# Packed attention and SwiGLU on one core: batch 0 as a written program, with plain fp32 products in its first four chunks

## The chip, the core and the metric

The kernel runs on one core of a Trainium2 chip. The kernel uses five engines, each with a queue of instructions of its own: TensorE (matmuls; the profile calls them PE, and the loads of the stationary operand PEld), VectorE (DVE), ScalarE (ACT), GpSimd (POOL) and SyncE (SP, which here issues nearly all DMA loads and stores). They wait for each other through semaphores. The metric is the device time of one execution in microseconds, lower is better.

## The reference

Eight batches of 576 tokens with 8 heads of 64 dimensions, and 32 pack queries per head and batch. Two attentions follow each other, then a SwiGLU layer:

```python
def sm_attn(qq, kk, vv):
    s = scale * np.matmul(qq, kk.transpose(0, 1, 3, 2))
    s = s - np.max(s, axis=-1, keepdims=True)
    a = np.exp(s)
    a = a / (np.sum(a, axis=-1, keepdims=True) + 1e-09)
    return np.matmul(a, vv)

p_packed = sm_attn(p, k, v)              # per head: 32 x 64
out = sm_attn(q, p_packed, p_packed)     # per head: 576 x 64
x = out, heads side by side              # 4608 tokens x 512
g = x @ w_gate                           # 512 x 1536
silu = g * (1.0 / (1.0 + np.exp(-g)))
return (silu * (x @ w_val)) @ w_out      # 1536 x 512
```

q, k, v and p arrive as fp32. The three weights arrive as 8-byte floats; the chip converts them to fp32 itself.

## The kernel before

**Folding.** The second attention ends with a product by the 32 packed values of each head, and the layer begins with a product by the gate and value weights. The kernel multiplies the two small factors first: M = (packed values) x (gate and value weights), per batch and per chunk of 128 of the 1536 hidden features (`m_part`, which does two chunks, a pair k, at once: `by_head`, L179). Then gate and value are products of M with the attention weights a2 alone (`gv_chunk`, L465). A chunk has a half a (256 tokens of an even batch) and a half b (the other 320); each half takes one PSUM tile for the gate and one for the value. ScalarE takes the silu of the gate tile (L472), VectorE multiplies it with the value tile (L478, and L481 for 64 tokens that are kept for a later product). The product h goes through the output weights into four PSUM accumulators.

**Precision.** A product is done either plainly in fp32 (each matmul shows as two records in the trace) or by three products of fp32r operands: both factors are split into a high part (a cast to fp32r, on ScalarE) and a low part (a subtraction, on VectorE), and low x high, high x low and high x high are added in PSUM. M is split into mh (L438) and ml (L421), a2 into a2h (L413) and a2l (L414). The output products of batches 1 to 7 are of three terms too (`out_mm`, L486), with output weights that are split once (`split_wout`, L144 and L145). Those of batch 0 are plain (`outs` in batch 0, L624).

**Batch 0 is different.** While it runs, the weights are converted: 12 chunks of gate and value weights (`convert_w`) and 6 pairs of chunks of output weights (`convert_wout`), a tile of 128 x 1024 each. A conversion (`f64_convert`) is two ScalarE passes (L111, L112) and then three VectorE passes (L113, L114, L115). It is a generator, so that its five steps can be put between other work one at a time. Beside this, batch 0 holds the whole attention of batch 1 (`aux_of`: scores, exponentials, transposes, packing, second scores and softmax), as each later batch holds that of its successor.

**Loads.** Raw weights, k and q of every batch go through one group of four buffers (`io_tile`). A load can be issued when the last reader of the tile that had its buffer is done.

**What sets the order.** TensorE's order is that of the program text throughout (the outer `manual_schedule`). In the preparation and in batch 0, VectorE's and ScalarE's order is that of the text too (the inner one). SP's order is chosen by the framework's planner. In batch 0 the text is a loop over the 24 halves: products of the half, its silu, some steps of conversions (`between`), its multiply, then the output products of the half five before (`LAG = 5`). M of pair k + 1 comes in the last half of pair k. Work in the list `late` (exponentials) goes behind a half's silu. After the loop come the last five output products, M of batch 1's first pair and the first two splits of output weights; the other ten splits lie in batch 1, two in each of five of its chunks.

## Time and profile before

| | |
|---|---|
| median of three runs | 796.53 us (795.73 to 796.65) |
| the profiled execution | 796.16 us |
| its span | 794.4 us |
| TensorE busy | 750.8 us (95%) |
| VectorE busy | 457.5 us (58%) |
| ScalarE busy | 376.2 us (47%) |
| first product of batch 0 | 23.29 us after the start of the span |
| last output product of batch 0 ends | 151.03 us |

The span is what the trace covers, from the first to the last instruction; the 1.8 us between it and the execution's time lie around it. A busy share is an average over the whole span: the slices of the page show TensorE at 40 to 90% in the first seven of 40 and above 90% after them. Matmuls are pipelined, so that the duration of one matmul (0.3 to 0.6 us in the groups) is longer than the distance to the next; where a stream of matmuls is to be priced, the chain of waits gives the distance, as it counts each stretch of time once. The granted clock of TensorE is printed for each stretch as a share of full speed.

### The profile page before, as it was taken

The page shows a single profiled execution, that of the slowest core. Times are in us where ns is not written, and L with a number is a line of the kernel's source. Part 1 is how long each engine was busy: PE and PEld are TensorE (multiplying, and loading weights), DVE is VectorE, ACT ScalarE, POOL GpSimd, SP SyncE. Part 2 cuts the span into 40 slices and gives each one's busy share as a digit, 9 for nine tenths or more (in the row PEclk, how much of TensorE's full clock was granted, in tenths as well). Part 3 has the DMA queues.
Part 4 walks back from the last instruction along what each step waited for, and adds up shares of the span by engine and source line. Part 5 has one row for each costly group of instructions (what it writes and reads, how often), then busy time and mean ns, then how long its engine had stood idle before and what let it go on. Part 6 is the DMA issues. An engine that isn't in the chain of part 4 may idle for free.

```text
span 794.4 us, 14060 instructions
## 1 busy us (share of the span) xinstructions
PE 750.8 (95%) x5750; PEld 590.0 (74%) x5750; DVE 457.5 (58%) x1002; ACT 376.2 (47%) x670; POOL 2.0 (0%) x13
## 2 busy tenths in 40 slices
PE   7478988999999999999999999999999999999998
PEld 5355555578777887878778787777888777888886
DVE  5785885565585554755475554754566454653434
ACT  3477673364462645464262643645362552643331
POOL 0000000000000000000000000000000000000000
PEclk9799999999999999999999999999999999999999
DMA  9564745320301212020211103010101000010001
GB/s 356 217 215 160 285 159 179 113 64 12 118 1 67 66 41 87 25 92 4 81 47 67 65 3 126 1 55 3 67 2 53 15 3 1 1 55 1 1 1 66
DMA packets 20000, 59.08 MB, mean 74 GB/s; under 512 B 5984, under 2 KB 7008, under 8 KB 17376
## 3 DMA queue, kind: packets, MB, share of 16 engines
q1 hardware_dynamic: 19792, 58.12, 20.5%
q8 instruction: 45, 0.74, 0.4%
q14 instruction: 19, 0.16, 0.1%
q10 hardware_dynamic: 144, 0.07, 0.0%
HBM read 48.69 MB, written 9.49 MB: 73 GB/s over the span
## 4 chain that ended last, share of the span: by engine, by line
PE 71%; ACT 10%; DVE 3%; issue 2%; ACTq 0%; DVEq 0%
PE gv L465 31%; PE acc L486 25%; PE aux L179 6%; PE aux L486 4%; ACT L472 4%; PE aux L349 2%; PE acc L624 2%; ACT sg L472 1%; DVE ml L421 1%; ACT mh L438 1%; ACT L297 1%; ACT hh L89 1%; ACT L392 1%; PE aux L284 1%; ACT s L392 1%
## 5 line engine op out<-in xcount | busy, mean ns | idle before, releaser
L465 PE MATMUL gv<-a2h,ml 128*128 128x256 f32 (+1 forms) x768 | 178.0, 313 | 24.3 <-ACT sg L472 13.7
L465 PEld LDWEIGHTS gv<-a2h,ml 128*128 128x128 f32 x768 | 129.7, 191 | 60.9 <-ACT sg L472 20.6
L472 ACT ACTIVATE sg<-gv 128x256 f32<-128x256 f32 x192 | 78.7, 410 | 192.0 <-PE gv L465 144.6
L465 PE MATMUL gv<-a2l,mh 128*128 128x256 f32 (+1 forms) x768 | 166.1, 298 | 0.0
L465 PE MATMUL gv<-a2h,mh 128*128 128x256 f32 (+1 forms) x768 | 165.7, 297 | 0.0
L478 DVE TENSOR_TENSOR hf<-gv,sg 128x256 f32<-128x256 f32 x168 | 70.7, 421 | 134.1 <-PE gv L465 117.8
L486 PE MATMUL acc<-wo_h,hl 128*128 128x512 f32 x336 | 136.6, 406 | 0.0
L486 PE MATMUL acc<-wo_l,hh 128*128 128x512 f32 x336 | 132.2, 393 | 0.0
L486 PE MATMUL acc<-wo_h,hh 128*128 128x512 f32 x336 | 131.6, 392 | 0.0
L465 PEld LDWEIGHTS gv<-a2l,mh 128*128 128x128 f32 x768 | 125.1, 191 | 0.3 <-DVE a2l L414 0.3
L465 PEld LDWEIGHTS gv<-a2h,mh 128*128 128x128 f32 x768 | 125.3, 192 | 0.0
L89 ACT CAST hh<-hf 128x256 fp32r<-128x256 f32 x168 | 67.8, 404 | 113.4 <-DVE hf L478 113.4
L95 DVE TENSOR_TENSOR hl<-hf,hh 128x256 fp32r<-128x256 f32 x168 | 71.1, 423 | 84.0 <-ACT hh L89 83.5
L486 PEld LDWEIGHTS acc<-wo_h,hl 128*128 128x128 f32 x336 | 63.2, 188 | 42.5 <-issue 34.4
L421 DVE TENSOR_TENSOR ml<-aux,mh 128x512 fp32r<-128x512 f32 (+1 forms) x96 | 61.2, 679 | 29.8 <-ACT mh L438 29.8
L486 PEld LDWEIGHTS acc<-wo_h,hh 128*128 128x128 f32 x336 | 63.1, 188 | 14.5
L486 PEld LDWEIGHTS acc<-wo_l,hh 128*128 128x128 f32 x336 | 63.3, 188 | 7.7
L179 PE MATMUL aux<-w,ppt 64*32 64x512 f32 (+1 forms) x768 | 52.7, 602 | 5.0 <-DVE w L115 3.3
L438 ACT CAST mh<-aux 128x512 fp32r<-128x512 f32 (+1 forms) x96 | 50.9, 583 | 8.1 <-PE aux L179 5.4
L472 ACT ACT_TABLE_LOAD x35 | 44.9, 1283 | 12.4 <-issue 11.6
L624 PE MATMUL acc<-wo_f,h 128*128 128x512 f32 x96 | 45.9, 598 | 0.9 <-DVE wo_f L115 0.9
L624 PEld LDWEIGHTS acc<-wo_f,h 128*128 128x128 f32 x96 | 16.6, 189 | 17.0 <-issue 15.2
(130 smaller groups left out, 631.2 us busy)
## 6 DMA issues: line engine op xcount, KB each, us to landing
st<-in_wgv SPq DMA_DIRECT2D x12, 1024.0 KB, 6.4
k_t<-in_kT SPq DMA_DIRECT2D x16, 576.0 KB, 4.8
q_t<-in_qT SPq DMA_DIRECT2D x16, 576.0 KB, 5.0
out<-ot SPq DMA_DIRECT2D x36, 256.0 KB, 2.1
v_t<-in_vq SPq DMA_DIRECT2D x6, 1280.0 KB, 5.7
st<-in_wout SPq DMA_DIRECT2D x6, 1024.0 KB, 4.8
v_t<-in_v SPq DMA_DIRECT2D x2, 1024.0 KB, 10.0
p_t<-in_pT SPq DMA_DIRECT2D x7, 64.0 KB, 1.8
```

Of the source, the lines that this page charges most:

```text
L89: e.copy(dst, src)
L95: lo.tensor_tensor(dst_l, src, dst_h.bitcast(F32), op=ALU.subtract)
L179: nc.tensor.matmul(outs[par][32 * hp : 32 * hp + 32], lhs(r, hp), rhs(r, hp), start=True, stop=True)
L349: nc.tensor.matmul(p_p[D * par : D * par + D, NP * hp : NP * hp + NP], v_t[:, par, hp, k, :], a1[:, par, hp, k, :], start=(k == 0), stop=( ...
L392: pin(nc.scalar.activation(x, x, AF.Exp, scale=SCALE))
L421: nc.vector.tensor_tensor(*lows.pop(0), op=ALU.subtract)
L438: nc.scalar.copy(mh[at], src)
L465: nc.tensor.matmul(pg[:, :n], m_[:, g, f, s * P : (s + 1) * P], a_[:, g, off : off + n], start=(i == 0), stop=(i == 5),)
L472: nc.scalar.activation(sg[:, :n], pgs[0][:, :n], AF.Silu)
L478: nc.vector.tensor_tensor(hf, pgs[1][:, o : o + 256], sg[:, o : o + 256], op=ALU.mult)
L486: nc.tensor.matmul(acc[:, :], h_[:, c : c + P], w_[fc // 2][:, fc % 2], start=(fc == 0 and i == 0), stop=(fc == NFC - 1 and i == 2),)
L624: nc.tensor.matmul(accs[2 * is_b + c], half(i)[:, c * P : c * P + P], wos[fc // 2][:, fc % 2], start=(fc == 0), stop=(fc == NFC - 1),)
```

## The change

The order of batch 0 is written out as text. In `run`, every word is one step: `g5` the products of half 5, `S5` its silu, `H5` its multiply, `O5` its output products, `M2.0` or `M2.2` M of pair 2 for its first or for both chunks (pair 6 stands for the first pair of batch 1), `L` the low parts of M, `W7:2` and `V2:1` so many steps of the conversion of gate and value chunk 7 and of output pair 2, `w7` and `v2` their loads, `a0` a low part of a2, `p3` a split of an output weight, `x` the next step of batch 1's attention, `q1` and `k2` loads of batches 1 and 2.

- Halves 0 to 7 (chunks 0 to 3) are products of one plain fp32 term: M is copied to SBUF without a split, and a2 is used as it comes from its transposes (`a2f`). From chunk 4 on there are three terms, in the order high x high, high x low, low x high. The parts of a2 are made ahead of half 7.
- The first four halves change their order: a of chunk 0, a of chunk 1, b of chunk 0, b of chunk 1. M of the first two pairs is done chunk by chunk.
- The two ScalarE passes of a conversion stand behind the silu of a half, ahead of the half in which VectorE's passes follow.
- An output product comes four halves after its half, and directly behind the products (and the M) of a half.
- The loads have two groups (rings) of two buffers, and SP's order is that of the text. The first load of an output weight and k of batch 1 move ahead of gate and value chunk 3 and of v of batch 1.
- 18 warm-up matmuls stand ahead of the first product in place of 10.
- Six output weights are split at the end of batch 0, the other six in chunks 1 to 6 of batch 1, one in each.

The diff, cut:

```diff
-    def io_tile(shape, dtype, name):
-        return pool.tile(shape, dtype, tag="io", bufs=4, name=name)
-    def f64_load(src):
-        st = io_tile([P, 1024, 2], I32, "st")
+    def io_tile(ring, shape, dtype, name):
+        return pool.tile(shape, dtype, tag=f"io{int(ring)}", bufs=2, name=name)
+    def f64_load(src, ring):
+        st = io_tile(ring, [P, 1024, 2], I32, "st")
...
+        sts[fc] = f64_load(wgv[fc], 0 if fc in (2, 5, 8, 10) else 1)
...
+        sts["out", k] = io_tile(k in (0, 3), [P, 1024, 2], I32, "st")
...
+        k_t = io_tile(0, [P, 2, NHP, HS], F32, "k_t")
         if b == 0:
-            qs[b] = io_tile([P, 2, NHP, HS], F32, "q_t")
+            qs[b] = io_tile(0, [P, 2, NHP, HS], F32, "q_t")
...
+            qs[b] = io_tile(1, [P, 2, NHP, HS], F32, "q_t")
...
+    def m_part(b, k, fcs, low=True, parts=("mh", "ml")):
+        plain = len(parts) == 1
         if (b, k) not in ms:
-            ms[b, k] = tuple(pool.tile([P, NPAR, 2, 2 * P], F32R, tag=t, bufs=2, name=t) for t in ("mh", "ml"))
-        mh, ml = ms[b, k]
+            dt = F32 if plain else F32R
+            ms[b, k] = tuple(pool.tile([P, NPAR, 2, 2 * P], dt, tag=t, bufs=2, name=t) for t in parts)
+        mh = ms[b, k][0]
...
+            if not plain:
+                lows.append((ms[b, k][1][at], src, mh[at].bitcast(F32)))
...
-        with tc.manual_schedule(engines={mybir.EngineType.DVE, mybir.EngineType.Activation}):
+        with tc.manual_schedule(
+            engines={mybir.EngineType.DVE, mybir.EngineType.Activation, mybir.EngineType.SP}
+        ):
...
-            load_v(1)
-            load_w(3)
-            load_k(1)
...
-            m_part(0, 0, slice(0, 1), low=False)
+            m_part(0, 0, c0, parts=("mh",))
             s2_max(0, c0)
             s2_exp(0, c0)
-            m_lows()
-            next(w1)
-            next(w1)
+            next(s2)
+            load_k(1)
+            load_wout(0)
+            warm_up(18)
+            steps(1, 2)
+            a2f = pool.tile([P, NPAR, S], F32, tag="a1", bufs=1, name="a2f")
+            def back(c):
+                for par in range(NPAR):
+                    nc.vector.transpose(a2f[:, par, c * HS : (c + 1) * HS], st2[0][0][:, c, par])
             s2_sums(0, c0)
             s2_scale(0, c0)
-            low = s2_back(0, 0)
-            run_all(s2)
-            warm_up(10)
-            low()
-            s2_max(0, c1)
-            s2_exp(0, c1)
-            next(w1)
-            next(w1)
-            s2_sums(0, c1)
-            s2_scale(0, c1)
-            low = s2_back(0, 1)
+            back(0)
...
+            order = [(0, 0), (1, 0), (0, 1), (1, 1)] + [divmod(i, 2) for i in range(4, 2 * NFC)]
+            PLAIN = 2
+            held = {}
+            def gv(i):
+                fc, is_b = order[i]
+                off, n = (NA, NB) if is_b else (0, NA)
+                k, f = divmod(fc, 2)
+                if k < PLAIN:
+                    terms = ((ms[0, k][0], a2f),)
+                else:
+                    (mh, ml), (ah, al) = ms[0, k], a2[0]
+                    terms = ((mh, ah), (mh, al), (ml, ah))
+                held[i] = [ps_gv.tile([P, 512], F32, tag="gv", name="gv") for _ in range(2)]
+                for s in range(2):
+                    todo = [(m_, a_, g) for m_, a_ in terms for g in range(NPAR)]
+                    for j, (m_, a_, g) in enumerate(todo):
+                        nc.tensor.matmul(
+                            held[i][s][:, :n], m_[:, g, f, s * P : (s + 1) * P], a_[:, g, off : off + n],
+                            start=(j == 0), stop=(j == len(todo) - 1),
+                        )
...
+            def a2_high():
+                s2_a2(0)
+                for c in range(2):
+                    at = (slice(None), slice(None), slice(c * HS, (c + 1) * HS))
+                    nc.scalar.copy(a2[0][0][at], a2f[at])
+            def a2_low(c):
+                at = (slice(None), slice(None), slice(c * HS, (c + 1) * HS))
+                nc.vector.tensor_tensor(a2[0][1][at], a2f[at], a2[0][0][at].bitcast(F32), op=ALU.subtract)
...
-            gv_chunk(0, 0, False, nothing, half(0), first_a)
...
+            gv(0)
+            s2_max(0, c1)
+            s2_exp(0, c1)
+            run("S0 W1:2 V0:1 W1:1 w3")
+            load_v(1)
+            run("M0.1")
+            s2_sums(0, c1)
+            run("V0:1 H0")
+            s2_scale(0, c1)
+            back(1)
+            run("g1 V0:1 S1 W2:1 H1 g2 V0:1 S2 W2:1 V0:1 w4 H2 g3 S3 W3:1 x O0 W2:1 H3 W2:1 W3:1 x O1 W2:1 w5 v1 M1.0")
+            run("O2 g4 S4 W4:1 W3:2 H4 g5 S5 W4:1 W3:1 w6 M1.1 W4:1 H5 x g6 S6 W5:1 W4:2 w7 H6 W5:1")
+            a2_high()
+            run("a0 g7 S7 V1:1 a1 W5:1 H7 W5:2 v2 M2.2 O3 V1:1 W6:1 L W6:1")
+            for words in (
+                "g8 S8 W7:2 V1:2 W6:1 H8 V1:1 w8 W6:1 O4",
+                "g9 S9 V2:2 W6:1 w9 H9 W7:1 V2:1 O5",
+                "g10 S10 x x W7:1 H10 W7:1 v3 O6",
+                "g11 S11 W8:1 M3.2 H11 V2:1 L W8:1 V2:1 w10 O7",
+                "g12 S12 W9:2 W8:1 H12 W8:1 x O8",
+                "g13 S13 V3:2 W8:1 H13 W9:1 V3:1 v4 O9",
+                "g14 S14 x W9:1 H14 W9:1 w11 O10",
+                "g15 S15 W10:1 M4.2 H15 V3:1 L W10:1 V3:1 q1 x O11",
+                "g16 S16 W11:2 W10:1 H16 W10:1 x O12",
+                "g17 S17 V4:2 x W10:1 H17 W11:1 V4:1 v5 O13",
+                "g18 S18 x W11:1 H18 x W11:1 O14",
+                "g19 S19 M5.2 H19 V4:1 L V5:2 V4:1 k2 x O15",
+                "g20 S20 x H20 V5:1 O16",
+                "g21 S21 x H21 x V5:1 O17",
+                "g22 S22 x H22 V5:1 O18",
+                "g23 S23 M6.2 H23 x L O19",
+                "O20 x p0 O21 x p1 O22 p2 p3 O23 p4 p5",
+            ):
+                run(words)
...
-                    if b == 1 and fc > 1 and count[0] in (3, 7):
-                        split_wout(fc - fc % 2 + count[0] // 7) if fc % 2 == 0 else None
+                    if b == 1 and 1 <= fc <= 6 and count[0] == 7:
+                        split_wout(fc + 5)
```

More of the change, by code (lines that the diff above doesn't have):

```diff
@@ L449, in h_split, with gv_chunk @@
         return hh, hl
-    def gv_chunk(b, fc, is_b, fill, kept=None, between=lambda: None):
+    def gv_chunk(b, fc, is_b, fill):
         odd = b % 2
@@ L474, in gv_chunk @@
             late.pop(0)()
-        between()
-        hf = pool.tile([P, 256], F32, tag="hf", bufs=2, name="hf") if kept is None else kept
+        hf = pool.tile([P, 256], F32, tag="hf", bufs=2, name="hf")
         o, o4 = (64, 0) if is_b and odd else (0, 256)
@@ L574, in tile_pack_attention_swiglu, with steps @@
             s1 = s1_post(0, True)
-            w0, w1 = convert_w(0), convert_w(1)
+            conv = {}
+            def steps(key, n=9):
+                if key not in conv:
+                    conv[key] = convert_wout(key[1]) if isinstance(key, tuple) else convert_w(key)
+                for _ in range(n):
+                    next(conv[key], None)
             for _ in range(4):
                 next(s1)
-            for _ in range(4):
-                next(w0)
+            steps(0, 4)
             next(s1)
-            run_all(w0)
+            steps(0)
             run_all(s1)
-            load_v(1)
-            load_w(3)
-            load_k(1)
             s2_tiles(0)
-            s2_a2(0)
             c0, c1 = (slice(c, c + 1) for c in range(2))
@@ L627, in outs @@
                     )
-                    yield
-            def nothing():
-                pass
-            conv = {}
-            def steps(key, n):
-                if key not in conv:
-                    conv[key] = convert_wout(key[1]) if isinstance(key, tuple) else convert_w(key)
-                for _ in range(n):
-                    next(conv[key], None)
-            def first_a():
-                run_all(w1)
-                low()
-            gv_chunk(0, 0, False, nothing, half(0), first_a)
@@ L719, in tile_pack_attention_swiglu @@
-            steps(("out", 5), 3)
-            load_k(2)
-            load_v(2)
-            for i in range(2 * NFC - LAG, 2 * NFC):
-                while late:
-                    late.pop(0)()
-                run_all(outs(i))
-                next(aux, None)
-                if i == 2 * NFC - 2:
-                    m_part(1, 0, both)
-                    split_wout(0)
-                    split_wout(1)
-            for _ in aux:
-                pass
-            load_q(2)
+            def a2_high():
[3 more added lines that the diff above has]
+                    nc.scalar.copy(a2[0][0][at], a2f[at])
@@ new lines, in a2_low, with attention @@
+            def a2_low(c):
+                at = (slice(None), slice(None), slice(c * HS, (c + 1) * HS))
+                nc.vector.tensor_tensor(a2[0][1][at], a2f[at], a2[0][0][at].bitcast(F32), op=ALU.subtract)
+            def attention():
+                yield from s1_scores(1, False)
+                yield
+                s1_exp(1, 0)
+                yield
+                s1_exp(1, 1)
+                yield
+                yield from s1_post(1)
+                s2_tiles(1)
+                yield from s2_scores(1)
+                s2_a2(1)
+                s2_max(1, c1)
+                yield
+                s2_exp(1, c1)
+                s2_max(1, c0)
+                yield
+                s2_exp(1, c0)
+                yield
+                for c in (c1, c0):
+                    s2_sums(1, c)
+                    yield
+                    s2_scale(1, c)
+                    low = s2_back(1, c.start)
+                    yield
+                    low()
+                yield
@@ new lines, in load_next, with run @@
+            def load_next(b):
+                load_k(b)
+                load_v(b)
+                load_q(b)
+            at1 = attention()
+            def run(program):
+                for word in program.split():
+                    op, arg = word[0], word[1:]
+                    if op in "WV":
+                        k, n = (int(x) for x in arg.split(":"))
+                        steps(k if op == "W" else ("out", k), n)
+                    elif op == "M":
+                        k, f = (int(x) for x in arg.split("."))
+                        nb, k = divmod(k, NFC // 2)
+                        plain = not nb and k < PLAIN
+                        m_part(nb, k, both if f == 2 else slice(f, f + 1), False, ("mh",) if plain else ("mh", "ml"))
+                    elif op == "x":
+                        next(at1, None)
+                    elif op == "L":
+                        m_lows()
+                    else:
+                        {"g": gv, "S": silu, "H": hmul, "O": outs, "w": load_w, "v": load_wout, "a": a2_low,
+                         "p": split_wout, "q": load_q, "k": load_next}[op](int(arg))
```

85 lines of the change are left out of this document (15 added, 70 removed).

## The prediction

> **What bounds the kernel now.** I began with the table of stretches (columns: from:to in us; busy time of TensorE matmuls, TensorE weight loads, VectorE, ScalarE and GpSimd, each with its count; granted TensorE clock; share and GB/s of the DMA engines).
>
> ```profile
> 16.00:150.60 134.60, 108.06 (x720) 67.12 (x704) 95.18 (x154) 76.61 (x105) 0.20 (x1) 0.95 0.57 204
> 23.30:26.50 3.20, 3.20 (x12) 2.69 (x12) 3.13 (x5) 0.68 (x1) 0.00 (x0) 0.50 0.98 383
> 26.50:32.50 6.00, 0.08 (x1) 0.00 (x0) 5.25 (x8) 2.32 (x3) 0.00 (x0) 0.78 0.38 134
> 32.50:38.00 5.50, 5.38 (x34) 4.03 (x34) 1.47 (x4) 2.35 (x6) 0.00 (x0) 0.60 0.48 185
> 38.00:40.60 2.60, 0.00 (x0) 0.00 (x0) 2.18 (x5) 0.79 (x1) 0.00 (x0) 0.93 0.00 0
> 40.60:43.80 3.20, 3.14 (x13) 3.17 (x14) 2.61 (x4) 2.60 (x3) 0.00 (x0) 0.52 0.33 67
> 69.30:150.60 81.30, 73.70 (x460) 43.87 (x460) 57.01 (x90) 42.25 (x57) 0.20 (x1) 1.00 0.52 186
> 150.60:249.00 98.40, 95.47 (x743) 77.17 (x743) 62.61 (x142) 49.77 (x93) 0.21 (x1) 1.00 0.16 56
> 336.80:433.00 96.20, 94.84 (x742) 77.01 (x742) 54.30 (x129) 44.12 (x81) 0.20 (x1) 1.00 0.17 60
> ```
>
> From batch 1 on, TensorE is busy 97% of the time and sets the pace. Batch 0 (16 to 150.6) is another regime: TensorE 108 of 134.6 us, some of it at half clock, VectorE 95, neither full. TensorE stands still 26.50 to 32.50 and 38.00 to 40.60, and after each pause its next products run at 0.50 to 0.60 clock. So only batch 0 and the first part of batch 1 can move.
>
> Then the timeline and the chain that ended last (start, duration, what), for what ends TensorE's pauses and what a unit of its work costs.
>
> ```profile
> 17.61 2.50 PE L549 MATMUL warm_ps<-ident 128*128 128x128 f32 x20
> 19.66 0.75 DVE L399 TENSOR_REDUCE r<-s 128x18 f32<-128x576 f32 x1
> 21.75 0.78 DVE L411 STREAM_TRANSPOSE t<-s 128x576 f32<-128x576 f32 x1
> 22.45 0.44 DVE L372 STREAM_TRANSPOSE s<-gv_aux 128x288 f32<-128x288 f32 x1
> 23.29 0.80 PE L465 MATMUL gv<-a2h,ml 128*128 128x256 f32 x2 [3.18 <-ACT a2h L413]
> ...
> 40.66 0.77 PE L465 MATMUL gv<-a2h,ml 128*128 128x256 f32 x2 [2.71 <-DVE t L481]
> 60.79 0.60 PE L226 MATMUL aux<-ident,t 128*128 128x128 f32 x4
> 75.00 1.88 PE L624 MATMUL acc<-wo_f,h 128*128 128x512 f32 x4
> 76.81 1.73 PE L241 MATMUL aux<-v_t,a 128*32 128x64 f32 x80
> 91.66 0.72 PE L179 MATMUL aux<-q_t,ppt 64*32 64x288 f32 x16
> 103.28 1.09 PE L179 MATMUL aux<-w,ppt 64*32 64x512 f32 x16 [1.48 <-DVE w L115]
> 106.61 0.38 PE L465 MATMUL gv<-a2h,ml 128*128 128x256 f32 x1 [1.18 <-DVE ml L421]
> ```
>
> The bracket is the pause before it and its releaser: a2h from ScalarE, the last VectorE multiply of the half before, a weight that VectorE hasn't converted, a low part of M that VectorE hasn't subtracted. Most of these go back to VectorE or to the order in which ScalarE and VectorE take things; none is a load.
>
> ```profile
> 133.43 1.44 PE gv L465 x12
> 134.86 1.72 PE acc L624 x4
> 148.10 1.02 PE aux L179 x16
> 149.12 1.91 PE acc L624 x4
> 151.03 0.12 PE gv L465
> ...
> 175.69 1.75 PE gv L465 x12
> ```
>
> Prices on a warm TensorE: a half's gate and value products by three terms 1.44 us (a, 256 tokens) or 1.75 (b, 320), its four output records 1.72, one M for two chunks 1.02. Two plain fp32 products of 512 columns are those four records, so one costs 0.86, or 0.43 per 256 columns. The last output product of batch 0 ends at 151.03; I follow that landmark.
>
> **The change part by part.** Durations on the other engines (last number before the bar's end: mean ns):
>
> ```profile
> L478 DVE TENSOR_TENSOR h<-gv,sg 128x256 f32<-128x256 f32 x24 | 10.1, 421 | 11.9 <-PE gv L465 7.4 <-ACT sg L472 4.4
> L481 DVE TENSOR_TENSOR t<-gv,sg 128x64 f32<-128x64 f32 x96 | 20.4, 212 | 0.0
> L113 DVE TENSOR_SCALAR w<-w 128x1024 f32<-128x1024 f32 x12 | 8.2, 681 | 1.4 <-ACT w L111 1.3
> L114 DVE SCALAR_TENSOR_TENSOR w<-w,st 128x1024 int32<-128x1024 int32 x12 | 14.6, 1221 | 1.1 <-ACT st L112 0.4
> L115 DVE SCALAR_TENSOR_TENSOR w<-st,w 128x1024 int32<-128x1024 int32 x12 | 14.6, 1213 | 0.2
> L111 ACT ACTIVATE w<-st 128x1024 f32<-128x1024 f32 x12 | 13.8, 1152 | 0.0
> L112 ACT ACTIVATE st<-st,minus_two 128x1024 f32<-128x1024 uint32 x18 | 22.4, 1242 | 0.0
> L421 DVE TENSOR_TENSOR ml<-aux,mh 128x512 fp32r<-128x512 f32 x94 | 60.4, 685 | 26.7 <-ACT mh L438 26.7
> L438 ACT CAST mh<-aux 128x512 fp32r<-128x512 f32 x94 | 50.3, 587 | 5.0 <-PE aux L179 2.3
> L472 ACT ACT_TABLE_LOAD x35 | 44.9, 1283 | 12.4 <-issue 11.6 <-DVE h L478 0.2
> L388 DVE TENSOR_TENSOR s<-s,r 128x576 f32<-128x576 f32 x16 | 12.1, 758 | 0.6
> L145 DVE TENSOR_TENSOR wo_l<-wo_f,wo_h 128x512 fp32r<-128x512 f32 x12 | 8.2, 691 | 0.9
> ```
>
> *Plain products (chunks 0 to 3).* Eight halves go from 1.44 or 1.75 to four plain products each, 4 x 0.43 = 1.72 or, by 320/256, 2.15. That adds 4 x (0.28 + 0.40) = 2.7 us of TensorE, in a stretch where TensorE waits. Taken away: four low parts of M (4 x 0.69 = 2.7 us of VectorE) and the wait for a2h and a2l; the splits of a2 still come, before chunk 4. ScalarE's casts of M become copies of the same shape, taken at the casts' 0.59.
>
> *First product.* The first half's sums start at 19.66 now, and what stands ahead of them keeps its length: the second half's transposes (2 x 0.44) take the place of the low parts of M. From the sums to the scaled weights are 2.1 us (19.66 to 21.75); then come two transposes of 288 columns, 0.85. So the product starts at 22.6, not 23.29. The ten warm-up products become 18: 36 records, at the 0.125 us of the 20 records of 2.50, from 17.6 to 22.1. They cost nothing, as TensorE waits till 22.6; were the chain shorter by more than 0.5, they would be the bound, with up to 4.5 us.
>
> *Start to the first use of the second converted output weight.* VectorE executes in program order, so I add up its list from 22.6 up to the last step of that conversion ("V1"), for which output product 4 waits: seven conversions (W1 to W5, V0, V1) at 0.68 + 1.22 + 1.22 = 3.1 each, 21.9; nine h multiplies, four with a tail, 9 x 0.42 + 4 x 0.21 = 4.6; the second half's maximum, sums, scaling and transposes 4.3 (five passes of 576 columns at 0.76 and small ones); maxima of batch 1's scores 1.9 (four at the 0.44 of 288 columns); two a2 splits 1.5; the low parts of one M 1.3; a first step of W6 0.7. Sum 36.2. To it come the waits that I find going along the three queues with these prices, where VectorE is free and what it needs is not there: 1.75 for batch 1's first scores, which stand behind half 3's products on TensorE (34.75 to 36.5); 2.1 for half 4's products behind W2's last step and M (43.8 to 45.9); 1.15 for ScalarE's second pass of W4 (47.55 to 48.7); 2.15 at M of chunks 4 and 5, where W5's last step, M and ScalarE's cast follow each other (59.15 to 61.3; the 1.48 and 1.18 pauses above are this chain); 0.3 for W6. 7.45 together. And the clock: TensorE pauses about 3.0 us after half 0 (for W1) and 4.8 before that M. The row of 38.00 says that a pause of 2.6 us suffices: 0.52 clock for the next 3.2 us. Half 1's products then take 1.72 longer, 0.5 of it under a VectorE step: 1.2; the M 1.0 longer. So 22.6 + 36.2 + 7.45 + 2.2 = 68.5 for output product 4; it starts at 75.00 now.
>
> The Trainium skill ("TensorE: Matmul & The Clock Gate", Part 1) has the clock fall only after an idle window of about 3.4 us. The 2.6 us pause here contradicts that; by the rule the pauses of 3.0 and (below) 2.7 us would be free and the sum 2.2 us lower.
>
> *Rounds 8 to 23.* From output product 4 TensorE has left: halves 9 to 23, 8 x 1.75 + 7 x 1.44 = 24.1; 20 outputs 34.4; four M 4.1; of batch 1's attention, transposes 1.6 (two of four records at 0.60, one smaller), packing 1.73, one more transpose 0.3, two score sets of 0.72: 5.0. Sum 67.5. Now, from 75.00: 14 halves 22.3, outputs 34.4, M 4.1, attention 3.4, 64.2 of the 76.0 to 151.03, so 11.8 us are waits. What waits do the new rounds leave? Per round I summed the engines' lists: TensorE 3.2 to 4.9 us; VectorE exceeds it in round 8 (V1 and half of W6; counted above) and round 19 (5.9 against 4.5: two M low parts, the V4 rest, maximum); ScalarE only where a change of table meets an M (round 11: 1.28, two passes 2.4, two casts 1.2 and a silu, 5.2 against 4.5). Going along: 1.4 in round 11 (the casts of M stand behind a table load and a W8 pass, and half 12 behind the casts); 1.85 in round 15 (transposes of batch 1 wait for a PSUM buffer that the low part of M frees, and output 11 stands behind them); 0.9 in round 18 (second scores, until the first are transposed out of PSUM); 1.0 in rounds 19 and 20 (low parts of M, V4); 0.85 in round 21 (half 20's multiply stands behind the second maximum); 1.0 for the clock after a 2.7 us pause between half 8 and output 4. Sum 7.0. What ScalarE gains by going ahead is inside this: its silu stands first in its round, with the passes behind it.
>
> So the landmark falls at 68.5 + 67.5 + 7.0 = 143.0 instead of 151.03: 8.0 us.
>
> *Splits of the output weights.* The first six move from batch 1 (four) to the end of batch 0 (two were there). In the tail VectorE has some 10 us (6 x 0.69 of splits, the low parts of M, the second half of a2) beside 1.02 + 5 x 1.72 = 9.6 us of products after half 23: covered; uncovered the four added ones would cost 2.8. Batch 1 takes 98.40 now, batch 3 without splits 96.20; of these 2.2 us I give back four tenths, 0.9 (bounds 0 and 2.2).
>
> *Loads.* All loads now stand in SP's queue in program order, in two rings of two buffers. One is issued when the conversion two back in its ring ends, or later, when a load ahead of it on SP waits. Their leads over first use, along the queues: W3 7.0 us, W11 7.8, W5 9, V3 and W10 10, V2, W4, W8 11, others more; k and q of batches 1 and 2 have over 5. From batch 1 on k and q have a ring each, and either tile is read a batch ahead of the load that takes its buffer: 0. What a load takes:
>
> ```profile
> DMA to landing us min/median/max: 4.8/5.1/13.7
> ```
>
> Median 5.1, so all are hidden; the 13.7 I put down to the first 26 us, where the engines are full (0.98 in the second row of stretches). Cost 0; uncovered it is rival 3.
>
> The profiled execution took 796.16 us (span 794.4, so 1.76 around it), 0.37 below the median of 796.53. 796.16 - 8.0 - 0.9 = **787.3**.
>
> **The rivals.** (1) *The waits stay.* ScalarE and VectorE remain strict queues with the same conversions in them; if rounds 9 to 23 wait 11.8 us as now and not 7.0: 792.1. For it: the M, cast, low part chain is unchanged. Against: outputs follow four halves late and fill what waited for weights. (2) *VectorE is denser than its durations.* Back to back, its instructions start before the last one's duration is over (21.75 + 0.78 = 22.53, the next at 22.45). With 0.08 for half of some 55 instructions, 2.2 go from the 36.2, and half of the 7.0 could go: 781.6. (3) *Slower: loads come late in two rings.* ScalarE takes passes in program order, so a late load holds the silu behind it and so TensorE. At 10 us per landing the leads lack 3.0 + 2.2 + 1 = 6 us: 793.5. At 12 us 5 + 4.2 + 3 + 2 x 2 + 3 x 1 = 19: 806. From about 11 us it is slower than before. Against: the stretches quoted from 32.5 to 150.6 show DMA shares of 0 to 0.52. (4) *Nothing comes of it*: the gain up to output 4 is taken back in the rounds by waits that I can't see (queues deeper by 8 us): 795 to 798.
>
> **How the numbers follow.** Forecast 55% (784 to 791), waits stay 17%, denser VectorE 14%, late loads 8%, nothing 6%. A measurement tells 0.2%, 1.6 us, from no change. Faster: the first three, 86%, less 1 for their tails; same 5%; slower 10%. The range reaches to rival 2 less the clock terms (781) and to rival 1 with one late load of 2 us (794); it leaves out late loads, nothing, and some of the edge.
>
> **What would show it.** First product near 22.6 in records of a plain product; TensorE's clock dipping near 27 to 32 and 55 to 65; output product 4 at 67 to 70, released by VectorE's last step of a conversion; landmark at 141 to 146; 1 to 2 us pauses in the rounds with M (11, 15, 19), none ended by a DMA; batch 1 at 97 to 98.4 us; batches 2 to 7 as they are. The prediction is wrong if ScalarE waits for loads, if output 4 starts after 73, or if the rounds take over 80 us.

## The result, and the profile after

The changed kernel takes **785.47 us** (median, 785.09 to 786.35), the kernel before beside it 796.14 (795.73 to 796.65): a ratio of 0.9867, with the 95% interval 0.985 to 0.9884. The forecast was 787.3, in a range of 781 to 794. The profiled execution took 786.35 us, with a span of 784.6; against the 796.16 and 794.4 of before that is 9.8 us less by both.

The busy rows of the profile's page, after (engine, busy us, share of the span, instructions), and the granted clock in 40 slices:

```profile
PE 753.5 (96%) x5750; PEld 590.1 (75%) x5750; DVE 453.0 (58%) x998; ACT 374.0 (48%) x670; POOL 2.0 (0%) x13
...
PEclk9997999999999999999999999999999999999999
```

TensorE is busy 2.7 us longer than before (750.8). So what fell is time in which it stands. The chain that ended last, after (start, duration, what):

```profile
133.20 8.78 PE acc L663 x20
141.98 3.28 PE gv L469 x24
...
231.31 8.16 PE aux L489 x36
239.47 3.94 PE gv L469 x30
```

The last output product of batch 0 ends at 133.20 + 8.78 = 141.98 us; this is the landmark, 151.03 before. Batch 1 ends at 239.47, 249.00 before (its row of the stretches in the prediction ends there). Its length is 97.49 us against 97.97. What follows takes 784.6 - 239.47 = 545.13 against 545.4. So batch 0 gives 9.05 us, batch 1 0.48, the other six 0.27: the 9.8.

Inside batch 0, the timeline of TensorE after (the bracket is the pause before the row and what ended it):

```profile
22.45 1.97 PE L637 MATMUL gv<-a2f,mh 128*128 128x256 f32 x8 [0.48 <-DVE a2f L611]
...
27.33 1.00 PE L180 MATMUL aux<-w,ppt 64*32 64x256 f32 x16 [2.91 <-DVE w L116]
...
59.37 1.96 PE L180 MATMUL aux<-w,ppt 64*32 64x512 f32 x16 [5.19 <-DVE w L116]
...
68.27 3.60 PE L663 MATMUL acc<-wo_f,h 128*128 128x512 f32 x4 [1.72 <-DVE wo_f L116]
```

First product 22.45 (before 23.29), output product 4 at 68.27 (75.00), landmark 141.98 (151.03): the three stretches give 0.84, 5.89 and 2.32 us. The last two are not like for like: one more half stands behind output product 4 than before, so that 3.3 us of priced work (67.5 and 64.2 in the prediction) went from the second stretch to the third. The pauses of 2.91 and 5.19 us wait for VectorE's last step of W1 and of W5. Stretches after (columns as in the prediction):

```profile
16.00:141.98 125.98, 110.92 (x721) 67.29 (x706) 93.73 (x154) 77.01 (x110) 0.20 (x1) 0.95 0.59 214
22.45:68.27 45.82, 34.03 (x188) 18.82 (x188) 33.90 (x55) 28.38 (x41) 0.00 (x0) 0.89 0.57 210
27.30:32.50 5.20, 4.68 (x28) 3.17 (x29) 3.98 (x10) 4.22 (x6) 0.00 (x0) 0.67 0.80 287
59.30:62.70 3.40, 3.33 (x18) 1.09 (x19) 0.67 (x2) 1.29 (x3) 0.00 (x0) 0.50 0.67 201
68.30:71.90 3.60, 3.60 (x5) 1.52 (x6) 2.28 (x2) 0.18 (x1) 0.00 (x0) 0.53 0.70 241
68.27:141.98 73.71, 71.05 (x449) 43.95 (x450) 54.06 (x88) 45.10 (x65) 0.20 (x1) 0.98 0.56 200
```

The last of these stretches before, from its output product 4 to its landmark:

```profile
75.00:151.03 76.03, 68.43 (x428) 39.38 (x426) 51.90 (x85) 38.45 (x52) 0.20 (x1) 1.00 0.55 197
```

From output 4 on TensorE stands for 73.71 - 71.05 = 2.66 us; before it stood for 7.60. The granted clock is 0.67 and 0.50 behind the two long pauses and, from 68.30, 0.53 behind a short one.

### The profile page after: what moved, and what is told of

It reads as the page before. It is cut to its first block, busy times and chain, and to the rows that moved or that the text cites. A ratio compares the mean times of both kernels' runs of the same rounds, so it can differ in the third digit from the quotient of the medians.

```text
span 784.6 us, 14057 instructions
## 1 busy us (share of the span) xinstructions
PE 753.5 (96%) x5750; PEld 590.1 (75%) x5750; DVE 453.0 (58%) x998; ACT 374.0 (48%) x670; POOL 2.0 (0%) x13
## 4 chain that ended last, share of the span: by engine, by line
PE 78%; ACT 11%; DVE 4%; issue 2%; DVEq 0%; ACTq 0%
PE gv L469 31%; PE acc L489 25%; PE aux L180 7%; PE acc L663 5%; PE aux L489 4%; ACT L476 4%; PE gv L637 3%; PE aux L350 2%; DVE ml L422 1%; ACT sg L476 1%; ACT hh L89 1%; ACT L393 1%; ACT mh L441 1%; ACT L298 1%; PE aux L285 1%
## 5 line engine op out<-in xcount | busy, mean ns | idle before, releaser
L469 PE MATMUL gv<-a2h,ml 128*128 128x256 f32 (+1 forms) x672 | 149.6, 304 | 7.5 <-ACT sg L476 6.2
L476 ACT ACTIVATE sg<-gv 128x256 f32<-128x256 f32 (+1 forms) x168 | 68.9, 410 | 171.8 <-PE gv L469 129.6
L469 PE MATMUL gv<-a2h,mh 128*128 128x256 f32 (+1 forms) x672 | 144.0, 296 | 0.0
L469 PE MATMUL gv<-a2l,mh 128*128 128x256 f32 (+1 forms) x672 | 143.9, 295 | 0.0
L469 PEld LDWEIGHTS gv<-a2h,ml 128*128 128x128 f32 x672 | 112.7, 188 | 32.5 <-ACT sg L476 11.4
L469 PEld LDWEIGHTS gv<-a2h,mh 128*128 128x128 f32 x672 | 108.4, 190 | 0.0
L469 PEld LDWEIGHTS gv<-a2l,mh 128*128 128x128 f32 x672 | 108.2, 189 | 0.0
L422 DVE TENSOR_TENSOR ml<-aux,mh 128x512 fp32r<-128x512 f32 x92 | 59.1, 684 | 20.0 <-ACT mh L441 20.0
L441 ACT CAST mh<-aux 128x512 fp32r<-128x512 f32 x92 | 49.2, 587 | 11.3 <-PE aux L180 8.7
L663 PE MATMUL acc<-wo_f,h 128*128 128x512 f32 x96 | 49.0, 642 | 1.7 <-DVE wo_f L116 1.7
L663 PEld LDWEIGHTS acc<-wo_f,h 128*128 128x128 f32 x96 | 17.5, 198 | 22.6 <-issue 20.3
```

The costliest lines, as they stand in the source:

```text
L422: nc.vector.tensor_tensor(*lows.pop(0), op=ALU.subtract)
L441: nc.scalar.copy(mh[at], src)
L469: nc.tensor.matmul(pg[:, :n], m_[:, g, f, s * P : (s + 1) * P], a_[:, g, off : off + n], start=(i == 0), stop=(i == 5),)
L476: nc.scalar.activation(sg[:, :n], pgs[0][:, :n], AF.Silu)
L663: nc.tensor.matmul(accs[2 * is_b + c], half(i)[:, c * P : c * P + P], wos[fc // 2][:, fc % 2], start=(fc == 0), stop=(fc == NFC - 1),)
```

## The experiments

The theory: the gain has two parts. Up to output 4, TensorE waits for VectorE's list (conversions W1 to W5, V0, V1), from which the plain products took work; from there on, outputs that come later relative to the conversions and a denser order shorten the waits. Loads cost nothing, the splits of the output weights a half microsecond. Rivals: the gain comes from ScalarE's head start, from the order of the loads, or from M's place and the order of the terms. O4 below is the start of output product 4; the landmark is worked out as above. Behind each time stand its lowest and highest, and its ratio to the kernel before as timed beside it (medians of 796.79 to 797.05 us in these sets, 796.14 in that of the result); a difference of two kernels is that of their medians.

**Undo the plain products.** `plain_off` gives chunks 0 to 3 three terms; a2 and M are split where they come, and the written order stays.

```diff
+            s2_a2(0)
...
-            m_part(0, 0, c0, parts=("mh",))
+            m_part(0, 0, c0)
...
+                nc.scalar.copy(a2[0][0][at], a2f[at])
+                nc.vector.tensor_tensor(a2[0][1][at], a2f[at], a2[0][0][at].bitcast(F32), op=ALU.subtract)
...
-            PLAIN = 2
+            PLAIN = 0
...
-            a2_high()
-            run("a0 g7 S7 V1:1 a1 W5:1 H7 W5:2 v2 M2.2 O3 V1:1 W6:1 L W6:1")
+            run("g7 S7 V1:1 W5:1 H7 W5:2 v2 M2.2 O3 V1:1 W6:1 L W6:1")
```

> The changed kernel with three fp32r terms from the first chunk on (M of chunks 0 to 3 split, a2 split directly behind its transposes). Theory (the order lists of the engines set batch 0): the first product comes 1.4 us later (cast 0.67, low part 0.75), VectorE's list up to output product 4 grows by eight low parts of 256 columns, 8 x 0.42 = 3.4, and TensorE saves 2.7 us in a stretch in which it waits anyway; output 4 at 72 to 73 instead of 68.3, time 789 to 790.5. Rival (the plain products are the gain): 794 to 796. Rival (four passes of fp32 cost what they say, TensorE being the bound there): 783.

Measured 788.73 us (787.9 to 789.45), 0.9892 [0.9869, 0.9916]. Timeline and chain of this kernel:

```profile
24.63 0.55 PE L641 MATMUL gv<-a2h,mh 128*128 128x256 f32 x2 [2.08 <-ACT a2h L614]
```

```profile
136.26 8.78 PE acc L667 x20
```

The first product comes 2.2 us later than after the change (1.4 was expected), O4 at 73.02, 4.75 later, and the landmark at 145.04, 3.06 later. Between the first product and O4 VectorE is busy 35.98 us and not 33.90: with the later start these are 4.3 of the 4.75. Behind O4 1.6 us come back, since output 4 runs at full clock here (1.98 us and not 3.60). In the median the plain products bring about 3.3 us (788.73 - 785.47), about a third of the gain; as output 4 alone moves by 1.6 us with the clock, this share is rough. The rest stays with the other edits.

**Undo ScalarE's head start.** In `scalar_late` the two ScalarE passes of a conversion stand directly ahead of its first VectorE pass; VectorE's order is untouched.

```diff
-            run("S0 W1:2 V0:1 W1:1 w3")
+            run("S0 W1:2 W1:1 w3")
...
-                "g12 S12 W9:2 W8:1 H12 W8:1 x O8",
+                "g12 S12 W8:3 H12 W8:1 x O8",
...
```

> The changed kernel with the two ScalarE passes of each conversion directly ahead of its first VectorE pass, in the same half, instead of half a chunk earlier. Theory (VectorE's and ScalarE's lists in order): VectorE waits for two passes, 2.3 us, wherever no other work of its own stands between; in about half of 16 conversions, of which a part is idle time of VectorE anyway: 7 to 14 us more, 792 to 800. Rival (VectorE is not full, 54 of 74 us after output 4, so the place of ScalarE's passes costs little): 785 to 787.

Measured 799.64 us (798.42 to 801.4), 1.0031 [1.0017, 1.0045]: 0.3% over the kernel before. The waits of VectorE in batch 0 of this kernel (us in total, times, longest):

```profile
DVE w L114 <- ACT w L112: 14.9, 7, 5.1
DVE wo_f L114 <- ACT wo_f L112: 8.0, 4, 3.8
```

After the change neither of the two waits at all (0.0 us in the groups). O4 falls to 77.93, the landmark to 153.96. Without the head start the whole gain is gone. It doesn't follow that the head start is new: before, the same first VectorE pass waits 1.3 us in all for ScalarE (the L113 row in the prediction). It is a condition of the gain, which the loop before mostly met too.

**Undo SP's written order.** `sp_planner` leaves SP out of the inner `manual_schedule`, so that the planner orders the loads again.

```diff
-            engines={mybir.EngineType.DVE, mybir.EngineType.Activation, mybir.EngineType.SP}
+            engines={mybir.EngineType.DVE, mybir.EngineType.Activation}
```

> The changed kernel with SP's order chosen by the framework again, and the two rings kept. Theory (loads have leads of 7 us and more over 4.9 us of landing): 785 to 787. Rival (the written order of the loads is a part of the gain): over 788.

Measured 787.69 us (787.37 to 788.09), 0.9879 [0.9859, 0.9899]: 2.2 us over the changed kernel, where I had expected none (the rival had said over 788). The timelines of SP, ScalarE and TensorE in this kernel:

```profile
14.78 0.33 SPq L163 DMA_DIRECT2D v_t<-in_v  x1
...
20.05 0.38 SPq L132 DMA_DIRECT2D st<-in_wout  x1
...
30.27 1.12 ACT L112 ACTIVATE wo_f<-st 128x1024 f32<-128x1024 f32 x1 [2.99 <-DMA st<-in_wout]
...
31.70 8.63 PE L637 MATMUL gv<-a2f,mh 128*128 128x256 f32 x24 [2.94 <-ACT mh L441]
```

After the change:

```profile
18.79 0.38 SPq L132 DMA_DIRECT2D st<-in_wout  x1
...
27.36 1.15 ACT L112 ACTIVATE wo_f<-st 128x1024 f32<-128x1024 f32 x1 [0.85 <-DMA st<-in_wout]
27.72 0.42 SPq L163 DMA_DIRECT2D v_t<-in_v  x1
```

And in `warm10` (below), which keeps the written order:

```profile
20.05 0.38 SPq L132 DMA_DIRECT2D st<-in_wout  x1
...
27.68 1.16 ACT L112 ACTIVATE wo_f<-st 128x1024 f32<-128x1024 f32 x1 [0.18 <-DMA st<-in_wout]
```

The planner puts v of batch 1 ahead of the first load of an output weight. That load is issued 1.26 us later than after the change, which isn't v's doing: in `warm10` it is issued at 20.05 as well. In both TensorE's clock was 0.50 from 14 to 18 us, where after the change it was 1.00, and the second scores, ahead of this, took longer (0.68 us each in `warm10`, 0.43 after the change). What v does is the landing: ScalarE's pass can start 10.2 us after the issue, and 7.6 after it in `warm10`; from 18.8 to 27.4 the DMA engines' share is 1.02 here and 0.81 there. ScalarE's pass waits 2.99 us, the copy of M stands behind it in the queue, and TensorE behind the copy. O4 comes at 71.35, the landmark at 143.37. This is rival 3's mechanism, at one load.

**Undo the two rings.** `one_group` keeps SP's order, with one group of four buffers.

```diff
-        return pool.tile(shape, dtype, tag=f"io{int(ring)}", bufs=2, name=name)
+        return pool.tile(shape, dtype, tag="io", bufs=4, name=name)
```

> The changed kernel with one group of four buffers instead of two rings of two, loads in the same written order. The load of W4 then waits for W2's conversion instead of V0's, about 7 us later, and lands about 1 us after ScalarE wants it; the other leads stay over 5 us. Theory (loads hidden): 785 to 787. Rival (the rings give the leads): over 788.

Measured 785.47 us (785.1 to 786.37), 0.9853 [0.9831, 0.9876], O4 68.29, landmark 141.89. As expected, the rings are worth nothing that shows.

**Undo the moved splits, and the warm-ups.** `splits_before` splits two output weights at the end of batch 0 and ten in batch 1, as before; `warm10` puts ten warm-up products in place of 18.

```diff
-                "O20 x p0 O21 x p1 O22 p2 p3 O23 p4 p5",
+                "O20 x p0 O21 x p1 O22 O23",
...
-                    if b == 1 and 1 <= fc <= 6 and count[0] == 7:
-                        split_wout(fc + 5)
+                    if b == 1 and fc > 1 and count[0] in (3, 7):
+                        split_wout(fc - fc % 2 + count[0] // 7) if fc % 2 == 0 else None
```

```diff
-            warm_up(18)
+            warm_up(10)
```

> The changed kernel with the splits of the output weights as before (two at the end of batch 0, ten in batch 1). Theory: batch 1 takes 98.0 instead of 97.5 us, and the end of batch 0 gains nothing, as the splits lie beside its output products: 785.8 to 786.5. Rival (the four splits at the end of batch 0 cost up to 2.8 us there): 783 to 785.

> The changed kernel with 10 warm-up products ahead of the first product instead of 18. Theory: TensorE waits for the conversion of W1 until 27.3 whatever half 0 takes, so half clock in half 0 (2 us more) ends before: 785 to 786.5. Rival (the warm clock is a part of the gain): 787 to 789.

Measured 785.5 us (784.13 to 787.17), 0.9855 [0.9832, 0.9878], and 785.48 (785.26 to 786.51), 0.9854 [0.9833, 0.9874]. The chain of `splits_before` holds the sizes:

```profile
68.31 1.98 PE acc L663 x4
...
131.56 8.78 PE acc L663 x20
...
230.17 8.16 PE aux L489 x36
```

Batch 1 runs from 140.34 to 238.33, 97.99 us: 0.5 longer than with the moved splits, as before the change. The landmark is 1.6 us earlier, though nothing ahead of it was changed but the text behind O19: output 4, at the same time, runs in 1.98 us and not in 3.60. In `warm10` the first product comes at 23.59 and O4 at 70.00, but output 4 takes 1.99 and the landmark is again at 142.03. The late first product isn't shown to come of the fewer warm-ups: the half clock from 14 to 18 us stands ahead of them. Nor does this execution show what half clock in half 0 would cost, as half 0 takes 1.89 us here too. So in the median both edits are worth less than the clock at output 4 moves by itself.

**Fill TensorE's pauses.** `pauses_filled` adds products whose results are not used: 8 behind half 0, 16 ahead of M of pair 2, 4 ahead of output 4 (the word `f` calls them).

```diff
+            def warm_fill(n):
+                t = ps()
+                for _ in range(n):
+                    nc.tensor.matmul(t[:, :P], ident, ident, start=True, stop=True)
...
             gv(0)
+            warm_fill(8)
...
-            run("a0 g7 S7 V1:1 a1 W5:1 H7 W5:2 v2 M2.2 O3 V1:1 W6:1 L W6:1")
+            run("a0 g7 S7 V1:1 a1 W5:1 H7 W5:2 v2 f16 M2.2 O3 V1:1 W6:1 L W6:1")
...
-                "g8 S8 W7:2 V1:2 W6:1 H8 V1:1 w8 W6:1 O4",
+                "g8 S8 W7:2 V1:2 W6:1 H8 V1:1 w8 W6:1 f4 O4",
```

> The changed kernel with warm-up products in three of TensorE's pauses: 8 behind half 0, 16 ahead of M of pair 2, 4 ahead of output product 4. Theory (a pause of 2 to 5 us halves the clock for what follows): M, output 3, output 4 and half 9 run at full clock; M ends 1 us earlier, output 4 takes 1.72 instead of 3.60: 782 to 783.5. Rival (only idle windows of 3.4 us count): one of the three pauses is that long, and what it slows lies beside VectorE's list: 784.5 to 786. Rival (the added products stand in the way): 786 to 788.

Measured 782.5 us (782.05 to 784.74), 0.9819 [0.9799, 0.9839]. Stretches of this kernel:

```profile
24.40:32.50 8.10, 6.63 (x50) 5.18 (x49) 7.59 (x13) 6.58 (x11) 0.00 (x0) 1.00 0.67 245
58.00:62.00 4.00, 3.81 (x29) 2.05 (x30) 1.98 (x5) 2.64 (x4) 0.00 (x0) 1.00 0.68 233
65.60:69.00 3.40, 3.32 (x15) 2.37 (x16) 2.38 (x3) 1.03 (x3) 0.00 (x0) 1.00 0.62 210
65.68:137.69 72.01, 69.38 (x449) 43.38 (x450) 54.06 (x88) 45.48 (x65) 0.20 (x1) 1.00 0.56 205
```

The clock is full behind all three pauses. O4 comes 2.6 us earlier, the landmark 4.3. Of these 4.3, output 4 itself gives 1.6 (1.98 us and not 3.60). In the median the lost clock was worth 3 us, as the theory had it; the rival by which only windows of 3.4 us count (784.5 to 786) is refuted.

**Fill the pauses of the kernel before.** `before_filled` adds 20 and 9 such products to the kernel before, at its pauses near 27 and 38 us.

```diff
             load_wout(0)
+            warm_fill(20)
...
+            def fill_1():
+                if first[0]:
+                    warm_fill(9)
+                first[0] = False
-            gv_chunk(0, 1, False, nothing, half(2), second_a)
+            gv_chunk(0, 1, False, fill_1, half(2), second_a)
```

> The kernel before with warm-up products in its two pauses near 27 and 38 us (20 and 9). Theory (what runs at half clock there stands partly on the path): 1 to 2.5 us off, 794 to 795.5 where before is 796.5. Rival (these stretches are set by VectorE and ScalarE alone): within 0.8 of before.

Measured 797.63 us (795.54 to 798.69), 0.9992 [0.9974, 1.0009]. Its clock there is 1.00 too:

```profile
26.50:38.00 11.50, 10.03 (x92) 8.97 (x90) 7.55 (x13) 5.48 (x8) 0.00 (x0) 1.00 0.45 172
```

In the median the full clock gave nothing that shows; 1 to 2.5 us were expected. The trace says where it went. Half 1 gains nothing: its products wait for ScalarE's silu of half 0 and start at 32.30 (32.57 before). The second part of half 2's products starts 1.5 us earlier (39.14 and not 40.66), M of the next pair too (45.49 and not 47.06). But now the clock falls behind that: from 48.3 to 54 us it is 0.52, where before it is 1.00. The landmark is at 150.30, 0.7 earlier. So in this execution the slow stretch came later instead of not at all, and took back some 0.8 of the 1.6 us gained. Whether the kernel before would gain from a full clock all through batch 0 isn't shown by this run.

**M's place and the order of the terms, put into the kernel before.** `before_order` puts M of the next pair behind both output products, and takes high x high first and low x high last in batch 0, as the changed kernel does.

```diff
-            for m_, a_ in ((ml, ah), (mh, al), (mh, ah)):
+            for m_, a_ in ((ml, ah), (mh, al), (mh, ah)) if kept is None else ((mh, ah), (mh, al), (ml, ah)):
...
-                for t, _ in enumerate(outs(i - LAG) if i >= LAG else ()):
-                    if t == 0 and slot == 3 and more:
-                        m_part(0, k + 1, both)
+                if i >= LAG:
+                    run_all(outs(i - LAG))
+                if slot == 3 and more:
+                    m_part(0, k + 1, both)
```

> The kernel before with two things of the changed text alone: M stands behind both output products of its half instead of between them, and the three terms of batch 0 come high x high first, low x high last. Theory (TensorE's waits for weights and low parts in the rounds, 1.48, 1.18, 1.84 us and others, are on the path, and work put into them is gained): 1.5 to 3 us off, 793.5 to 795 where before is 796.5. Rival (the wait moves to the next half): within 0.8 of before.

Measured 798.24 us (796.61 to 802.06), 1.0017 [0.9996, 1.0038]: no gain. From its output 4 to its landmark TensorE still stands for 7.0 us (7.60 before, 2.66 after). M waits 0.44 us for its weight where it waited 1.48, but the half behind it then waits 1.49 us for ScalarE's cast of M. So in the kernel before these two edits alone don't shorten the waits of the rounds; they move them.

**Plain products everywhere.** `plain_all` does all 24 halves of batch 0 plainly; a2 isn't split there.

```diff
...
-            PLAIN = 2
+            PLAIN = 6
...
-            a2_high()
-            run("a0 g7 S7 V1:1 a1 W5:1 H7 W5:2 v2 M2.2 O3 V1:1 W6:1 L W6:1")
+            run("g7 S7 V1:1 W5:1 H7 W5:2 v2 M2.2 O3 V1:1 W6:1 L W6:1")
```

> The changed kernel with plain fp32 products in all twelve chunks of batch 0 and no split of batch 0's a2 and M. Theory (plain products are worth their TensorE time only where TensorE waits): up to output product 4, VectorE's list loses 2.8 us of a2's and M's low parts and 3 to 4 us of waits for ScalarE's casts, so output 4 comes at 62 to 64; after it TensorE, which is the bound there, has 5.4 us more (8 x 0.28 + 8 x 0.40), less 1.5 to 2.5 of waits for low parts: 782 to 784.5. Rival (VectorE is the bound all through batch 0): 780 or less. Rival (TensorE's four passes decide): 787 or more.

Measured 786.58 us (785.47 to 788.42), 0.9858 [0.9833, 0.9884]: no gain over four chunks (782 to 784.5 expected). The timeline up to output 4, and the stretch from there to the landmark:

```profile
59.08 1.96 PE L180 MATMUL aux<-w,ppt 64*32 64x512 f32 x16 [3.20 <-DVE w L116]
...
67.43 1.98 PE L663 MATMUL acc<-wo_f,h 128*128 128x512 f32 x4 [2.07 <-DVE wo_f L116]
```

```profile
67.43:142.55 75.12, 73.76 (x389) 41.28 (x390) 50.91 (x82) 45.52 (x65) 0.20 (x1) 1.00 0.55 196
```

I had O4 at 62 to 64; it came at 67.43, since M of pair 2 still waits for W5, and V1 follows it. Behind it TensorE is busy 73.76 of 75.12 us: there the longer products are the bound.

**Write halves 3 to 15 more tightly.** `tight` keeps every step and moves VectorE's into its waits: the high parts of a2 ahead of W5, M of pair 2 chunk by chunk so that halves 8 and 9 don't wait for W5, and halves 9 and 10 ahead of output 4.

```diff
...
-            run("a0 g7 S7 V1:1 a1 W5:1 H7 W5:2 v2 M2.2 O3 V1:1 W6:1 L W6:1")
+            run("W5:1 a0 g7 S7 a1 M2.0 V1:1 W5:1 H7 O3 L g8 S8 V1:1 W5:2 v2 H8 g9 S9 V1:1 M2.1 W6:1 H9 V1:1 L V1:1 w8")
...
-                "g8 S8 W7:2 V1:2 W6:1 H8 V1:1 w8 W6:1 O4",
-                "g9 S9 V2:2 W6:1 w9 H9 W7:1 V2:1 O5",
-                "g10 S10 x x W7:1 H10 W7:1 v3 O6",
-                "g11 S11 W8:1 M3.2 H11 V2:1 L W8:1 V2:1 w10 O7",
+                "g10 S10 W6:1 H10 W6:3 w9 W7:2 O4 O5",
+                "g11 S11 V2:2 W7:2 H11 W7:1 v3 V2:1 O6 M3.2 O7 V2:1 L V2:1 w10",
...
```

> The changed kernel with another text for halves 3 to 15: VectorE steps are moved into the five places where VectorE waits up to output 4, a2's high parts come ahead of the second ScalarE pass of W5, M of pair 2 is done chunk by chunk so that halves 8 and 9 don't wait for W5, and half 10 stands ahead of output 4. Theory (VectorE's list with its waits sets the time of output 4, TensorE's list what follows): output 4 at 62 to 65 with one more half done, 777 to 781. Rival (ScalarE becomes the bound in rounds 10 to 14, where passes and exponentials crowd): 783 to 787.

Measured **779.44 us** (778.68 to 780.49), 0.9776 [0.9755, 0.9797]. Output 4 follows the products ahead of it without a pause, and TensorE has done two more halves by then:

```profile
63.10 0.40 PE L637 MATMUL gv<-a2h,ml 128*128 128x256 f32 x2
63.54 2.84 PE L663 MATMUL acc<-wo_f,h 128*128 128x512 f32 x6
```

The landmark is at 134.35. The 6.0 us hold the clock too: the changed kernel with its pauses filled has its landmark at 137.69, and of the pauses that were filled there `tight` has only the first left. `tight_filled` adds `warm_fill(8)` behind half 0, where the one pause of over 2 us is left.

> The kernel with the other text for halves 3 to 15, and eight warm-up products in the one pause of over 2 us that it has left, behind half 0. Theory (half 1 and half 2 then run at full instead of 0.7 clock): 1 to 1.7 us off 779.4, 777.7 to 778.5. Rival (half 1 lies beside VectorE's list): 779 to 779.8.

Measured **778.19 us** (778.09 to 778.21), 0.9753 [0.9727, 0.9779]: 7.3 us below the changed kernel, the fastest of all. From `tight` to this are 1.25 us, for a pause of 2.91 us; the times of the two, from two sets of runs, don't overlap, but the intervals of their ratios do.

## Why the prediction was right, and where it was off

The time, the place of the gain and the four points of the timeline came out as worked out. The forecast started from the profiled execution: 8.9 us were to come off it, 9.8 came; the landmark gave 1.0 more than forecast, batch 1 0.4 less, the other six batches 0.3. But in both sums inside batch 0 errors cancel, so that part of the closeness is luck.

- *First product*: 22.6 forecast, 22.45 measured. In the median the warm-ups cost nothing and bring nothing (`warm10`).
- *Output product 4*: 68.5 forecast, 68.27 measured, released by V1's last step as said. But two errors cancel here. The list of 36.2 us is right as a sum of durations (36.8 when the durations of the trace in this stretch are added), but too long as time: VectorE is busy 33.90 us from 22.45 to 68.27, since its instructions overlap when they follow each other. That is rival 2, which put 2.2 us on it. The waits and the clock, 7.45 + 2.2 = 9.65, are too short: 45.82 - 33.90 = 11.9. With the pauses filled the stretch takes 42.81 us (22.87 to 65.68), so that by this estimate about 3.0 of the 11.9 are the clock (2.2 forecast) and 8.9 waits (7.45). The timeline of VectorE after, in which a wait for a slow product holds the clock too:

```profile
37.43 0.82 DVE L198 TENSOR_REDUCE mx<-aux 128x1 f32<-128x288 f32 x2 [2.20 <-PE aux L180]
...
46.88 0.42 DVE L655 TENSOR_TENSOR h<-gv,sg 128x256 f32<-128x256 f32 x1 [2.64 <-PE gv L637]
...
54.34 1.43 DVE L676 TENSOR_TENSOR a2l<-a2f,a2h 128x576 fp32r<-128x576 f32 x2 [1.75 <-ACT a2h L672]
...
62.03 1.29 DVE L422 TENSOR_TENSOR ml<-aux,mh 128x512 fp32r<-128x512 f32 x2 [2.80 <-ACT mh L441]
```

  Forecast for the first, second and fourth: 1.75, 2.1, 2.15. The third, for ScalarE's cast of a2, I hadn't seen; the 1.15 for W4 did not come.
- *Rounds 8 to 23*: 67.5 of work and 7.0 of waits forecast; 73.71 measured, so 6.2. Of the 7.0, 1.0 was the clock behind the pause ahead of output 4, and 6.0 were waits. The runs part the two: with output 4 at full clock, the stretch from O4 to the landmark is 72.03 (`splits_before`), 72.01 (`pauses_filled`), 72.03 (`warm10`) and 72.02 us (`sp_planner`). So the clock cost 1.7 in the profiled execution, not 1.0. The other 4.5 are not all waits: TensorE stands for 2.66 us only, and 1.9 us are work that the sum of 67.5 didn't have (69.38 busy at full clock in `pauses_filled`). So here too two errors cancel: the waits were put at 6.0 and are 2.66, the work was put 1.9 too low. The forecast also read the 11.8 us of before as waits, where TensorE stands for 7.60. After the change these four waits are all:

```profile
84.26 0.38 PE L637 MATMUL gv<-a2h,ml 128*128 128x256 f32 x1 [0.18 <-DVE ml L422]
...
98.80 0.41 PE L227 MATMUL aux<-ident,t 128*64 128x128 f32 x2 [1.46 <-DVE ml L422]
...
112.22 1.08 PE L180 MATMUL aux<-q_t,ppt 64*32 64x288 f32 x16 [0.63 <-DVE s L373]
...
124.41 0.56 PE L637 MATMUL gv<-a2h,mh 128*128 128x320 f32 x2 [0.39 <-DVE h L655]
```

  The last three stand where I put them, in rounds 15, 18 and 21 (forecast 1.85, 0.9 and 0.85). Of the 1.4 of round 11 there is 0.18, of the 1.0 of rounds 19 and 20 nothing.
- *Clock*: that a pause of 3 us and less can halve it was right, but not each does (last section); the rule of the Trainium skill ("TensorE: Matmul & The Clock Gate", Part 1), by which only idle windows of about 3.4 us do, would have left nothing to fill behind half 0, where the 2.91 us pause is followed by 0.67. The measurement decides.
- *Splits*: 0.9 forecast for batch 1, 0.48 measured, and 0.5 by undoing them; inside the bounds of 0 and 2.2.
- *Loads*: 0 forecast. The rings are worth 0. The order is not: by the planner's order the kernel takes 2.2 us more, and its trace has one late load. The landing of 13.7 us that I put down to the full engines of the first 26 us was the warning: the first output weight's load is issued at 18.79, inside them, and has no slack. ScalarE still waits 0.85 us for it after the change, which the prediction named as a sign of being wrong; it cost nothing that shows, as in `one_group` ScalarE doesn't wait there and O4 comes at 68.29.
- *Rivals*: "the waits stay" is refuted (TensorE stands for 2.66 and not 7.60 us in the rounds), "nothing comes of it" too. "Denser VectorE" holds for the list, and more than half of the rounds' 6.0 us of waits went as it said, but not for the end: the longer waits ahead of O4 and the work that was priced too low took it back. "Late loads" holds for one load, under another order.

Which waits of the rounds went can be read from the traces: 4.23 of the 4.94 us are waits of TensorE for a converted weight. Before there were three (1.48 us at 103.28, in the prediction, and these two); after the change there is none from O4 on.

```profile
123.31 1.09 PE L179 MATMUL aux<-w,ppt 64*32 64x512 f32 x16 [1.84 <-DVE w L115]
...
142.68 5.42 PE L624 MATMUL acc<-wo_f,h 128*128 128x512 f32 x12 [0.91 <-DVE wo_f L115]
```

What stays open is which edit did it. M's place and the order of terms don't do it in the kernel before; outputs four halves late, directly behind the products, and the placed conversion steps were not parted by any run. So about two thirds of the gain belong to the written order as a whole, the order of the loads included. A general delay of the loads was not tried either.

## What to carry to other kernels

Where two engines hand work to each other in strict order, add up the list of the one that ends last, as union of its busy time and not as sum of durations, and then look for what stands in each of its waits: moving work into those (`tight`, 6.0 us, regained clock included) brought more than the cheaper arithmetic did (`plain_off`, 3.3 us). Filling TensorE's pauses with unused products brought 3.0 us in the changed kernel and nothing that shows in the kernel before, where the slow stretch came later instead; look in the trace where the clock falls next. A load issued while the DMA engines are full needs its place in the queue checked by itself.

## What the runs showed of the hardware

**The length of a short pause doesn't decide the clock behind it.** Output 4 behind a pause of 1.72 us ran in 3.60 us after the change (quoted above), and in `warm10`, behind the same pause, at full clock:

```profile
70.00 1.99 PE L663 MATMUL acc<-wo_f,h 128*128 128x512 f32 x4 [1.72 <-DVE wo_f L116]
```

With 2.53 us it took 2.40 (`one_group`), with 2.07 again 1.98 (`plain_all`). The length of the slow stretch differs too: behind a pause of 5.2 us and the same M, output 3 took 3.78 us after the change and 2.49 in `one_group`. The Trainium skill ("TensorE: Matmul & The Clock Gate", Part 1) says that the gate watches a window that runs freely, and that the point at which the clock rises depends on where in it the first matmul falls. The scatter here would fit such a window, but no run shows it. For a forecast this means a scatter of up to 1.7 us that no sum over the text resolves.

**A plain fp32 gate product costs per column what an output product does.** I priced it at 0.86 us per 512 columns from the output products, with no such gate product in the trace of before. The chain after has two halves, a and b, of four plain products each in one piece:

```profile
45.04 3.88 PE gv L637 x16
```

The forecast was 1.72 + 2.15 = 3.87.
